# Token mixing of three batches beside the last MoE, and channel mixing over all tokens in chunks of 384

## The chip, the cores and the metric

The kernel runs on one core of one Trainium2 chip. The metric is the device time of one execution in microseconds (us), as the median of several runs. A profile of one execution stands beside it.

## The reference

Three layers follow each other on 4 batches of 576 tokens. Cut to what matters:

```python
attn = softmax(causal(q @ k.T / 8 + min(-(cum_i - cum_j), 0))) @ v      # 4 batches, 8 heads, 64 wide
x    = attn as (4, 576, 512)

xk, xr = mu_k * x + (1 - mu_k) * x_prev,  mu_r * x + (1 - mu_r) * x_prev
k = maximum(xk @ w_k, 0)                                                # 512 -> 1024
x = sigmoid(xr @ w_r) * (k * k @ w_v)                                   # the "MoE" layer

h = maximum(x.transpose(0, 2, 1) @ w_tok1, 0) @ w_tok2                  # token mixing: 576 -> 256 -> 576
u = x + h.transpose(0, 2, 1)
out = u + maximum(u @ w_ch1, 0) @ w_ch2                                 # channel mixing: 512 -> 1536 -> 512
```

All inputs are float32. Token mixing needs all 576 tokens of its batch; channel mixing works on each token by itself.

## The kernel before

**Precision.** Most products are made of two parts per operand, a rounded high part and the remainder. `products` (L103) issues three matmuls for each pair of 128-row blocks: high by high, high by low, low by high. So every result that a later product reads is "split": ScalarE writes the high part and VectorE or GpSimd subtracts it to make the low part. A weight is split the same way on its first use, in pieces: `weight_load` (L538) brings a piece of 256 or 288 columns into a buffer of the ring `xt`, and `weight_split` (L550) takes three ScalarE, two VectorE and one GpSimd instruction to place its two parts. The ring `xt_p` (L83) has six buffers; the attention's output of the batch in work lies in four of them until the MoE's `mix` has read it.

**Stages.** Attention runs over 32 heads in items. The MoE of each batch is cut into units (`moe_units`, L507): for each of two chunks of 256 and 320 tokens there are 8 `up`, 4 `gate` and 8 half `down` units. They are spread over the attention items that follow, so that TensorE has matmuls beside the softmax. The MoE of the last batch has no attention left beside it; its units and a few of the one before form the list `queue` (L734). The MoE's result goes to DRAM (`y_d`).

**The mixer.** For each batch, `load_y` brings the result back, `y_transpose` turns half of the 512 channels at a time (five PSUM tiles, each copied by ScalarE and subtracted by VectorE, and then one small copy by DMA for the 64 rows of the fifth block), `tok1` makes the hidden layer of token mixing (H1), and `tok2` the second product, adds x and splits the sum into `U`. `ch1` makes 12 blocks of the hidden layer of channel mixing for one chunk, `ch2` the four blocks of the output. Both work on the chunks of 256 and 320 tokens of one batch. The first of these steps, for batch 0, stand among the last units of `queue`, at places given in `st` (L836); the later batches' token steps stand between the channel steps of the batch before. All these PSUM tiles come from `ps_m` with six buffers; `ps_d`, with two, serves the earlier stages and the first 14 units of `queue`.

**Memory.** The tokens' second weight `T2`, the transposed `YN` and `H1` lie in the memory of the MoE's weight `WK`. `C1`, the first channel weight, has its own. The second channel weight takes the memory of `WV` and `WR`. `U` and the hidden layer take that of the MoE's `XR`, `KK` and `XK`.

**Order.** A planner orders the instructions of each engine by priorities and its own times. `at(place)` (L68) gives what stands under it the priority of that place in the list of attention items; a smaller number goes first. Buffers are handed out in the same order.

```python
    def at(place):
        return tc.high_priority(tc.cur_priority - int(place * 1000))
    ...
    xt_p = ctx.enter_context(tc.tile_pool(name="xt", bufs=6))
    ...
    ps_d = ctx.enter_context(tc.tile_pool(name="ps_d", bufs=2, space=PSUM, reuse_waits="tile"))
```

## Time and profile before

| what | value |
|---|---|
| median of 3 runs (lowest to highest) | 914.5 us (913.0 to 916.4) |
| the profiled execution: its time, its span | 911.6 us, 909.7 us |
| mean granted clock of TensorE in it | 0.989 |
| TensorE matmuls | 6032 |

The span runs from the first to the last instruction of the profiled execution; its time has 1.9 us more around it. PE is TensorE's matmuls, PEld its weight loads, DVE VectorE, ACT ScalarE, POOL GpSimd, SP SyncE, which issues nearly all DMAs. A line number is that of the kernel before; L108 is the matmul in `products`, which all products share. Matmuls overlap, so the time between two starts says more than the duration of one. The granted clock is 1.00 at 2.4 GHz and 0.50 at 1.2 GHz. A tile that lies in the memory of another carries its name: `t<-WK` is token mixing, `c<-XR,C` the first channel product, `c<-KK,WV` and `c<-XK,WR` the second.

### The profile page before, as it was taken

What the parts mean: (1) busy time and instruction counts of PE and PEld (TensorE: products, weight loads), DVE (VectorE), ACT (ScalarE), POOL (GpSimd) and SP (SyncE); (2) the same over time, 40 slices, a digit from 0 to 9 for tenths busy, and PEclk for the clock granted to TensorE, in tenths of its full rate; (3) what the DMA queues carried; (4) which work ended last, traced back from release to release, by engine and by line L of the source; (5) the groups of instructions that cost most, each with busy time, mean ns of one, the idle gap of its engine ahead of it and who ended that gap; (6) DMA issues with size and microseconds to landing.
All of it is one profiled execution on the core that took longest, in us unless ns stands there. A gap on an engine that the chain in (4) does not pass through costs nothing.

```text
span 909.7 us, 17091 instructions
## 1 busy us (share of the span) xinstructions
PE 871.0 (96%) x6032; PEld 793.3 (87%) x6032; DVE 523.3 (58%) x1582; ACT 468.1 (51%) x1296; POOL 292.1 (32%) x405
## 2 busy tenths in 40 slices
PE   7879999999899999999999799999999999999998
PEld 4435778998689989989999699999999999999998
DVE  5796776777898577876468887532323223222220
ACT  4787867766776757768367967321212111211120
POOL 4574536644565526545143734100000000000000
PEclk9979999999999999999999999999999999999999
DMA  7943355456644435542034553500010001000000
GB/s 200 246 126 88 91 142 115 108 120 153 146 95 102 107 94 125 107 109 42 32 94 144 177 175 128 166 4 22 10 52 4 15 16 50 6 16 15 19 6 30
DMA packets 57222, 79.61 MB, mean 88 GB/s; under 512 B 6144, under 2 KB 36096, under 8 KB 57136
## 3 DMA queue, kind: packets, MB, share of 16 engines
q1 hardware_dynamic: 55264, 77.92, 32.8%
q8 instruction: 48, 0.79, 0.4%
q10 hardware_dynamic: 1872, 0.59, 0.3%
q14 instruction: 38, 0.31, 0.1%
HBM read 46.67 MB, written 10.03 MB: 62 GB/s over the span
## 4 chain that ended last, share of the span: by engine, by line
PE 65%; DMA 10%; DVE 9%; issue 7%; ACT 5%; POOL 3%; SPq 0%; ACTq 0%; POOLq 0%; DVEq 0%
PE c L108 32%; PE vd L108 6%; PE h L108 5%; PE t L108 4%; PE r L108 3%; PE pv L446 3%; PE t L398 3%; PE pv L384 2%; DMA X<-HL 2%; DMA raw<-in_moe_w_ch_dram 2%; PE s L357 2%; PE s L276 2%; DVE raw L555 1%; PE s L277 1%; DMA HL<-in_qk_dram 1%
## 5 line engine op out<-in xcount | busy, mean ns | idle before, releaser
L108 PE MATMUL c<-XR,C 128*128 128x320 f32 (+1 forms) x1152 | 156.2, 295 | 1.0 <-ACT XR L809 1.0
L108 PEld LDWEIGHTS c<-XR,C 128*128 128x128 f32 x1152 | 153.2, 188 | 2.0 <-ACT XR L809 1.2
L264 POOL TENSOR_SCALAR P<-P,sum 64x576 f32<-64x576 f32 (+4 forms) x160 | 107.1, 673 | 120.7 <-DVE sum L263 64.0
L108 PE MATMUL h<-XK,WK 128*128 128x256 f32 (+1 forms) x768 | 121.7, 301 | 2.7 <-DVE XK L464 1.5
L108 PE MATMUL vd<-KK,WV 128*128 128x256 f32 (+1 forms) x768 | 121.1, 300 | 2.3 <-POOL KK L476 1.6
L261 ACT ACTIVATE P<-P,mx 64x576 f32<-64x576 f32 (+4 forms) x160 | 95.9, 600 | 31.1 <-DVE mx L251 27.0
L108 PEld LDWEIGHTS h<-XK,WK 128*128 128x128 f32 x768 | 105.5, 188 | 7.0 <-DVE XK L464 2.1
L108 PEld LDWEIGHTS vd<-KK,WV 128*128 128x128 f32 x768 | 105.3, 188 | 5.8 <-POOL KK L476 2.8
L108 PE MATMUL c<-KK,WV 128*128 128x256 f32 (+1 forms) x768 | 106.5, 294 | 0.1
L108 PEld LDWEIGHTS c<-KK,WV 128*128 128x128 f32 x768 | 103.0, 188 | 0.4 <-DVE XK L785 0.4
L784 ACT ACTIVATE KK<-c 128x256 fp32r<-128x256 f32 (+1 forms) x64 | 26.1, 409 | 145.9 <-PE c L108 145.9
L251 DVE CUSTOM_DVE_ANT_0 P<-s,maskc 64x288 f32<-64x288 f32 (+4 forms) x160 | 74.9, 474 | 19.3 <-PE t L398 4.7
L826 DVE TENSOR_TENSOR u<-c,u 128x256 f32<-128x256 f32 (+1 forms) x32 | 14.5, 457 | 121.7 <-PE c L108 121.7
L785 DVE SCALAR_TENSOR_TENSOR KK<-c,KK 128x256 fp32r<-128x256 f32 (+1 forms) x64 | 29.1, 457 | 66.8 <-ACT KK L784 66.8
L108 PE MATMUL r<-XR,WR 128*128 128x320 f32 (+1 forms) x384 | 62.3, 304 | 0.9 <-ACT k L473 0.6
L75 ACT ACTIVATE raw<-raw 128x256 f32<-128x256 f32 (+2 forms) x101 | 46.8, 464 | 27.8 <-DMA raw<-in_moe_w_ch_dram 11.3
L476 POOL TENSOR_TENSOR KK<-k,KK 128x256 fp32r<-128x256 f32 (+1 forms) x64 | 54.6, 857 | 19.1 <-ACT k L475 18.3
L555 DVE SCALAR_TENSOR_TENSOR raw<-raw 128x256 int32<-128x256 int32 (+2 forms) x85 | 47.0, 553 | 22.0 <-ACT raw L554 19.3
L108 PEld LDWEIGHTS r<-XR,WR 128*128 128x128 f32 x384 | 54.8, 193 | 2.4 <-ACT k L473 0.8
L108 PE MATMUL c<-XK,WR 128*128 128x320 f32 (+1 forms) x384 | 55.8, 294 | 0.0
L398 PE MATMUL t<-ident,P 128*128 128x128 f32 (+1 forms) x360 | 53.5, 262 | 1.8 <-DVE PT L424 1.3
L556 DVE SCALAR_TENSOR_TENSOR raw<-raw 128x256 int32<-128x256 int32 (+2 forms) x85 | 53.1, 628 | 1.1
(109 smaller groups left out, 1525.7 us busy)
## 6 DMA issues: line engine op xcount, KB each, us to landing
X<-HL SPq DMA_DIRECT2D x72, 288.0 KB
raw<-in_moe_w_ch_dram SPq DMA_DIRECT2D x48, 256.0 KB
HL<-in_qk_dram SPq DMA_DIRECT2D x12, 576.0 KB
yt<-y_d SPq DMA_DIRECT2D x16, 288.0 KB
raw<-in_moe_w_k_dram SPq DMA_DIRECT2D x8, 512.0 KB
...
```

Of the source, the lines that this page charges most:

```text
L75: nc.scalar.activation(out=out, in_=in_, func=AF.Copy, scale=scale)
L108: nc.tensor.matmul(ps, a, b, start=first and i == 0, stop=last and i == n - 1)
L251: nc.vector.tensor_tensor_reduce(out=P[0:m, c0:c1], in0=ps[0:m, 0:c1 - c0], in1=maskc[0:m, 512 - q0 + c0:512 - q0 + c1], scale=-scale, sca ...
L261: nc.scalar.activation(out=P[0:m, 0:w], in_=P[0:m, 0:w], func=AF.Exp, bias=mx[0:m, x:x + 1], scale=-1.0, accum_out=sm[0:m, 0:1])
L264: nc.gpsimd.tensor_scalar(out=P[0:m, 0:w], in0=P[0:m, 0:w], scalar1=sm[0:m, 1:2], scalar2=1.0, op0=ALU.mult, op1=ALU.mult)
L398: nc.tensor.transpose(ps[0:r, p0 + m * k:p0 + m * k + m], P[0:m, 128 * k:128 * k + r], ident[0:m, 0:m])
L446: nc.tensor.matmul(ps[:, o:n], vv[0:r, k, :], pair[t], start=(k == 0 and t == 0), stop=(k == nk - 1 and t == 1),)
L476: nc.gpsimd.tensor_tensor(out=kk[:, 1, m, 0:n], in0=t[:, 0:n], in1=f32(kk[:, 0, m, 0:n]), op=ALU.subtract)
L555: nc.vector.scalar_tensor_tensor(out=low, in0=high, scalar=3, in1=low, op0=ALU.logical_shift_left, op1=ALU.bitwise_or)
L556: nc.vector.scalar_tensor_tensor(out=low, in0=high, scalar=-2 ** 31, in1=low, op0=ALU.bitwise_and, op1=ALU.bitwise_or)
L784: nc.scalar.activation(out=hi, in_=ps, func=AF.Relu)
L785: nc.vector.scalar_tensor_tensor(out=lo, in0=ps, scalar=0.0, in1=f32(hi), op0=ALU.max, op1=ALU.subtract)
```

## The change

Channel mixing no longer goes batch by batch. All 2304 tokens form one row, cut into six chunks of 384 (`CH`), so that a chunk can hold tokens of two batches (`spans`). For this `tok2` no longer splits its sum into `U`: it adds into the tile of x and stores u to a new DRAM tensor, `u_d`. `split_u` loads the four blocks of a chunk and splits them; `ch2` loads each block again as the addend and stores its part of the output.

Token mixing of batches 0 and 1 is listed step by step (`tok_steps`) and spread over the units of the last MoE, from the seventh on, six places later than its unit. Token mixing of batch 2 stands behind the last unit, that of batch 3 between the `ch1` steps of the first chunk. All token steps take their PSUM tiles from `ps_d`. Batch 1's x lies in the ring `xt`, that of the other batches in five buffers of its own.

The first channel weight is in two parts: `C1A`, 512 columns, in its own memory, and `C1B`, 1024 columns, in that of `WK`. `T2`, `YN` and `H1` get memory of their own, and the hidden layer and `U` a new pool in the MoE's place. The pieces of the token weights and of `C1A` enter at one per unit from the start, those of `C1B` at two per unit with the last 12 units, those of the second channel weight behind batch 2's token steps and the first `ch1` steps.

```diff
@@ -99,6 +99,7 @@
     ext_d = dram.tile([G, 4, 2, S], F32, name="ext_d")
     y_d = dram.tile([B, DM, S], F32, name="y_d")
+    u_d = dram.tile([B, DM, S], F32, name="u_d")
@@ -693,7 +694,7 @@
-    ap = ctx.enter_context(tc.tile_pool(name="act", bufs=1, reuse_waits="tile"))
+    ap_s, ap = open_pool(name="act", bufs=1, reuse_waits="tile")
@@ -734,48 +735,50 @@
     queue = [(n, acts) for n in sorted(todo) for acts in todo[n]]
     att.close()
     with tc.using_default_side("right"):
         mx_p = ctx.enter_context(tc.tile_pool(name="mx", bufs=1, reuse_waits="tile"))
-        yt_p = ctx.enter_context(tc.tile_pool(name="yt", bufs=KD // 2, reuse_waits="tile"))
     ps_m = ctx.enter_context(tc.tile_pool(name="ps_m", bufs=6, space=PSUM, reuse_waits="tile"))
-    C1 = mx_p.tile([128, 2, KD, DC], F32R, name="C1")
+    CH = 384
+    CA = 512
+    DH = DM // 2
+    yt = {}
+    def load_y(b):
+        for p in range(KD):
+            if b == 1:
+                t = xt_p.tile([128, 1 + S], F32, tag="xt", name="yt")[:, 0:S]
+            else:
+                t = mx_p.tile([128, S], F32, tag="yt", name="yt", bufs=5)
+            nc.sync.dma_start(out=t, in_=y_d[b, 128 * p:128 * p + 128, :])
+            yt[b, p] = t
+    load_y(0)
+    C1A = mx_p.tile([128, 2, KD, CA], F32R, name="C1A")
+    T2 = mx_p.tile([128, 2, KT, S], F32R, name="T2")
     T1 = mx_p.tile([128, 2, NS, DT], F32R, name="T1")
+    YN = mx_p.tile([128, 2, NS, DH], F32R, name="YN")
+    H1 = mx_p.tile([128, 2, KT, DM], F32R, name="H1")
+    C1B = WK.rearrange("p (t k f) -> p t k f", t=2, k=KD)
     c2a = WV.rearrange("p (t k f) -> p t k f", t=2, f=DM)
     c2b = WR.rearrange("p (t k f) -> p t k f", t=2, f=DM)
-    o = 0
-    T2 = WK[:, o:o + 2 * KT * S].rearrange("p (t k f) -> p t k f", t=2, k=KT)
-    o += 2 * KT * S
-    DH = DM // 2
-    YN = WK[:, o:o + 2 * NS * DH].rearrange("p (t k f) -> p t k f", t=2, k=NS)
-    o += 2 * NS * DH
-    H1 = WK[:, o:o + 2 * KT * DM].rearrange("p (t k f) -> p t k f", t=2, k=KT)
-    U = act["XR"]
-    def hid(t, k, n):
-        return act["KK"][:, t, k, 0:n] if k < KF else act["XK"][:, t, k - KF, 0:n]
+    def c1(t, k, m):
+        f = 128 * m
+        return C1A[:, t, k, f:f + 128] if f < CA else C1B[:, t, k, f - CA:f - CA + 128]
 
     def c2(t, k, ms):
         return c2a[:, t, k, ms] if k < KF else c2b[:, t, k - KF, ms]
-    yt = {}
-    def load_y(b):
-        for p in range(KD):
-            if p < KD // 2:
-                t = yt_p.tile([128, S], F32, tag="yt", name="yt")
-            else:
-                t = xt_p.tile([128, 1 + S], F32, tag="xt", name="yt")[:, 0:S]
-            nc.sync.dma_start(out=t, in_=y_d[b, 128 * p:128 * p + 128, :])
-            yt[p] = t
 
     def y_transpose(b, h):
         for i in range(NS):
             r = min(128, S - 128 * i)
-            ps = ps_m.tile([128, DH], F32, tag="d", name="yn")
+            ps = ps_d.tile([128, DH], F32, tag="d", name="yn")
             for p in range(KD // 2):
-                nc.tensor.transpose(ps[0:r, 128 * p:128 * p + 128], yt[h * (KD // 2) + p][:, 128 * i:128 * i + r], ident)
+                nc.tensor.transpose(ps[0:r, 128 * p:128 * p + 128], yt[b, h * (KD // 2) + p][:, 128 * i:128 * i + r], ident)
             nc.scalar.activation(out=YN[0:r, 0, i, :], in_=ps[0:r, :], func=AF.Copy)
             nc.vector.tensor_tensor(out=YN[0:r, 1, i, :], in0=ps[0:r, :], in1=f32(YN[0:r, 0, i, :]), op=ALU.subtract)
         nc.sync.dma_start(out=f32(YN[TAIL:2 * TAIL, 0, NS - 1, :]), in_=f32(YN[0:TAIL, 1, NS - 1, :]))
@@ -786,7 +789,7 @@
 
     def tok1(b, h):
         for m in range(KT):
-            ps = ps_m.tile([128, DH], F32, tag="d", name="t1")
+            ps = ps_d.tile([128, DH], F32, tag="d", name="t1")
             ms = slice(128 * m, 128 * m + 128)
             k = NS - 1
             products(ps, [(T1[:, 0, k, ms], T1[:, 1, k, ms], YN[:, 0, k, :], YN[:, 1, k, :]) for k in range(k)], last=False)
@@ -795,36 +798,53 @@
             ds = slice(DH * h, DH * h + DH)
             relu_split(ps, H1[:, 0, m, ds], H1[:, 1, m, ds])
 
-    ut = {}
-    def tok2(b, c):
-        cs = slice(*CHS[c])
-        n = width(c)
-        u = sm_p.tile([128, KD, n], F32, tag=f"u{c}", name="u")
+    def tok2(b, m):
+        ms = slice(128 * m, 128 * m + 128)
+        t = yt.pop((b, m))
+        for cs in (slice(0, S // 2), slice(S // 2, S)):
+            ps = ps_d.tile([128, S // 2], F32, tag="d", name="t2")
+            products(ps, [(H1[:, 0, k, ms], H1[:, 1, k, ms], T2[:, 0, k, cs], T2[:, 1, k, cs]) for k in range(KT)])
+            nc.vector.tensor_tensor(out=t[:, cs], in0=ps, in1=t[:, cs], op=ALU.add)
+        nc.sync.dma_start(out=u_d[b, ms, :], in_=t)
+    def tok_steps(b):
+        return [(load_y, b), (y_transpose, b, 0), (tok1, b, 0), (y_transpose, b, 1), (tok1, b, 1)] + [(tok2, b, m) for m in range(KD)]
+    def spans(i):
+        r, o = [], 0
+        while o < CH:
+            b, a = divmod(CH * i + o, S)
+            z = min(S, a + CH - o)
+            r.append((b, a, z, o))
+            o += z - a
+        return r
+    def load_u(i, m):
+        t = xt_p.tile([128, 1 + S], F32, tag="xt", name="ut")[:, 0:CH]
+        for b, a, z, o in spans(i):
+            nc.sync.dma_start(out=t[:, o:o + z - a], in_=u_d[b, 128 * m:128 * m + 128, a:z])
+        return t
+    def split_u(i):
         for m in range(KD):
-            ms = slice(128 * m, 128 * m + 128)
-            ps = ps_m.tile([128, n], F32, tag="d", name="t2")
-            products(ps, [(H1[:, 0, k, ms], H1[:, 1, k, ms], T2[:, 0, k, cs], T2[:, 1, k, cs]) for k in range(KT)])
-            nc.vector.tensor_tensor(out=u[:, m, 0:n], in0=ps, in1=yt[m][:, cs], op=ALU.add)
-            nc.scalar.activation(out=U[:, 0, m, 0:n], in_=u[:, m, 0:n], func=AF.Copy)
-            nc.vector.tensor_tensor(out=U[:, 1, m, 0:n], in0=u[:, m, 0:n], in1=f32(U[:, 0, m, 0:n]), op=ALU.subtract)
-        ut[b, c] = u
-    def ch1(c, m):
-        n = width(c)
+            t = load_u(i, m)
+            nc.scalar.activation(out=U[:, 0, m, :], in_=t, func=AF.Copy)
+            nc.vector.tensor_tensor(out=U[:, 1, m, :], in0=t, in1=f32(U[:, 0, m, :]), op=ALU.subtract)
+    def ch1(m):
+        ps = ps_m.tile([128, CH], F32, tag="d", name="c1")
+        products(ps, [(c1(0, k, m), c1(1, k, m), U[:, 0, k, :], U[:, 1, k, :]) for k in range(KD)])
+        relu_split(ps, HID[:, 0, m, :], HID[:, 1, m, :])
+    def ch2(i, m):
         ms = slice(128 * m, 128 * m + 128)
-        ps = ps_m.tile([128, n], F32, tag="d", name="c1")
-        products(ps, [(C1[:, 0, k, ms], C1[:, 1, k, ms], U[:, 0, k, 0:n], U[:, 1, k, 0:n]) for k in range(KD)])
-        relu_split(ps, hid(0, m, n), hid(1, m, n))
-    def ch2(b, c, m):
-        n = width(c)
-        ms = slice(128 * m, 128 * m + 128)
-        ps = ps_m.tile([128, n], F32, tag="d", name="c2")
-        products(ps, [(c2(0, k, ms), c2(1, k, ms), hid(0, k, n), hid(1, k, n)) for k in range(KC)])
-        u = ut[b, c]
-        nc.vector.tensor_tensor(out=u[:, m, 0:n], in0=ps, in1=u[:, m, 0:n], op=ALU.add)
-        nc.sync.dma_start(out=out[b, ms, CHS[c][0]:CHS[c][1]], in_=u[:, m, 0:n])
+        t = load_u(i, m)
+        ps = ps_m.tile([128, CH], F32, tag="d", name="c2")
+        products(ps, [(c2(0, k, ms), c2(1, k, ms), HID[:, 0, k, :], HID[:, 1, k, :]) for k in range(KC)])
+        nc.vector.tensor_tensor(out=t, in0=ps, in1=t, op=ALU.add)
+        for b, a, z, o in spans(i):
+            nc.sync.dma_start(out=out[b, ms, a:z], in_=t[:, o:o + z - a])
 
     def by_columns(pieces):
         return [p[x] for x in range(len(pieces[0])) for p in pieces]
@@ -832,62 +852,64 @@
     wq = []
     for k in range(NS):
         wq += weight(T1[:, 0, k:k + 1], T1[:, 1, k:k + 1], w_tok1, k)
-    wq += by_columns([weight(C1[:, 0, k:k + 1], C1[:, 1, k:k + 1], w_ch1, k) for k in range(KD)])
-    st = [14, 7, 5, 4, 1]
-    START = {}
-    for q, f in zip(st, ([load_y, 0], [y_transpose, 0, 0], [tok1, 0, 0], [y_transpose, 0, 1], [tok1, 0, 1])):
-        START.setdefault(q, []).append(f)
-    done = 0
+    for k in range(KT):
+        wq += weight(T2[:, 0, k:k + 1], T2[:, 1, k:k + 1], w_tok2, k)
+    wq += by_columns([weight(C1A[:, 0, k:k + 1], C1A[:, 1, k:k + 1], w_ch1[:, 0:CA], k) for k in range(KD)])
+    fill = tok_steps(0)[1:] + tok_steps(1)
+    nf = len(fill)
+    n0 = 6
     for x, (n, acts) in enumerate(queue):
-        if len(queue) - x == KF + KD:
-            for k in range(KT):
-                for p in weight(T2[:, 0, k:k + 1], T2[:, 1, k:k + 1], w_tok2, k):
-                    with at(N0 + n + 0.6):
-                        p()
+        left = len(queue) - x
+        if left == KF + KD:
+            wq += by_columns([weight(C1B[:, 0, k:k + 1], C1B[:, 1, k:k + 1], w_ch1[:, CA:], k) for k in range(KD)])
         if x == 14:
             act["ps"] = ps_m
         with at(N0 + n + 0.5):
             run(acts)
-            for f in START.get(len(queue) - x, []):
-                f[0](*f[1:])
-        if done <= x and wq:
-            done += 1
-            with at(N0 + n + 0.6):
-                wq.pop(0)()
+        for _ in range(1 if left > KF + KD else 2):
+            if wq:
+                with at(N0 + n + 0.6):
+                    wq.pop(0)()
+        while x >= n0 and fill and nf - len(fill) < nf * (x - n0 + 1) // (len(queue) - n0):
+            with at(N0 + n + 6):
+                run(fill[0:1])
+            fill.pop(0)
+    run(fill)
     st_s.close()
-    sm_p = ctx.enter_context(tc.tile_pool(name="sm2", bufs=1, reuse_waits="tile"))
-    ctx.enter_context(at(N0 + n + 2))
-    tok2(0, 0)
+    ap_s.close()
+    ch_p = ctx.enter_context(tc.tile_pool(name="ch", bufs=1, reuse_waits="tile"))
+    HID = ch_p.tile([128, 2, KC, CH], F32R, name="HID")
+    U = ch_p.tile([128, 2, KD, CH], F32R, name="U")
+    ctx.enter_context(at(N0 + n + 7))
     two = []
     for k in range(KC):
         W, kk = (c2a, k) if k < KF else (c2b, k - KF)
         two.append(weight(W[:, 0, kk:kk + 1], W[:, 1, kk:kk + 1], w_ch2, k))
     wq += by_columns(two)
-    for b in range(B):
+    def convert(n):
+        for _ in range(n):
+            if wq:
+                wq.pop(0)()
+    fill = tok_steps(2)
+    for f in fill:
+        run([f])
+        convert(1)
+    split_u(0)
+    last = tok_steps(3)
+    for i in range(B * S // CH):
         for m in range(KC):
-            ch1(0, m)
-            for _ in range(2):
-                if wq:
-                    wq.pop(0)()
-        tok2(b, 1)
+            ch1(m)
+            convert(2)
+            if i == 0 and m > 1 and last:
+                run([last.pop(0)])
+        run(last)
+        last = []
+        if i + 1 < B * S // CH:
+            split_u(i + 1)
         for m in range(KD):
-            ch2(b, 0, m)
-        if b + 1 < B:
-            load_y(b + 1)
-            y_transpose(b + 1, 0)
-        for m in range(KC):
-            ch1(1, m)
-            if b + 1 < B:
-                if m == 2:
-                    tok1(b + 1, 0)
-                if m == 3:
-                    y_transpose(b + 1, 1)
-                if m == 6:
-                    tok1(b + 1, 1)
-        if b + 1 < B:
-            tok2(b + 1, 0)
-        for m in range(KD):
-            ch2(b, 1, m)
+            ch2(i, m)
 
 # ---- launch: one core; inputs and outputs as the reference has them ----
```

## Rows read from the trace of the kernel before

**Rows 1.** The page's first part: busy time, share of span, instructions per engine.

```profile
PE 871.0 (96%) x6032; PEld 793.3 (87%) x6032; DVE 523.3 (58%) x1582; ACT 468.1 (51%) x1296; POOL 292.1 (32%) x405
```

**Rows 2.** The table of windows: busy by engine, granted clock, DMA share, GB/s.

```profile
460.00:480.00 20.00, 18.37 (x152) 17.55 (x151) 14.66 (x27) 14.25 (x42) 11.57 (x14) 1.00 0.24 69
...
505.00:510.00 5.00, 3.60 (x23) 3.07 (x21) 4.91 (x6) 4.54 (x15) 4.32 (x6) 1.00 0.34 100
510.00:515.00 5.00, 4.74 (x31) 4.36 (x31) 4.00 (x8) 5.00 (x17) 3.61 (x4) 1.00 0.56 179
515.00:520.00 5.00, 1.95 (x11) 1.26 (x10) 4.93 (x8) 5.00 (x17) 4.26 (x6) 0.89 0.46 127
520.00:525.00 5.00, 4.76 (x19) 4.33 (x18) 2.89 (x8) 3.15 (x9) 2.58 (x4) 0.50 0.83 243
```

**Rows 3.** TensorE's timeline, 456 to 547: start, us, instruction, count, idle before.

```profile
456.61 4.25 PE L108 MATMUL h<-XK,WK 128*128 128x256 f32 x36
...
516.77 0.44 PE L778 MATMUL yn<-ident,yt 128*128 128x128 f32 x2 [1.62 <-ACT e L488]
...
546.66 17.25 PE L108 MATMUL c<-XR,C 128*128 128x256 f32 x144 [0.97 <-ACT XR L809]
```

**Rows 4.** TensorE's timeline, 602 to 679: token and channel mixing.

```profile
602.80 1.58 PE L108 MATMUL t<-WK,T 128*128 128x256 f32 x12
...
606.90 8.97 PE L108 MATMUL c<-XR,C 128*128 128x320 f32 x60
...
615.70 3.04 PE L108 MATMUL t<-WK 128*128 128x256 f32 x24
...
618.58 3.69 PE L108 MATMUL c<-KK,WV 128*128 128x320 f32 x24
...
639.70 17.25 PE L108 MATMUL c<-XR,C 128*128 128x256 f32 x144
...
656.79 3.67 PE L108 MATMUL t<-WK 128*128 128x320 f32 x24
...
660.30 2.99 PE L108 MATMUL c<-KK,WV 128*128 128x256 f32 x24
...
677.27 1.25 PE L778 MATMUL yn<-ident,yt 128*128 128x128 f32 x10
...
678.28 5.53 PE L108 MATMUL c<-XR,C 128*128 128x320 f32 x36
```

**Rows 5.** TensorE's timeline during attention: score matmuls of 384 columns.

```profile
304.11 0.34 PE L276 MATMUL s<-X 128*128 128x384 f32 x1
...
304.46 1.63 PE L108 MATMUL h<-XK,WK 128*128 128x320 f32 x10
```

**Rows 6.** Groups by line and shape, ScalarE and VectorE, 440 to 910.

```profile
L75 ACT ACTIVATE raw<-raw 128x256 f32<-128x256 f32 x51 | 22.2, 435 | 18.0 <-DMA raw<-in_moe_w_ch_dram 11.3 <-DMA raw<-in_moe_w_tok_dram 4.9 <-POOL WV L560 1.6
...
L779 ACT ACTIVATE WK<-yn 128x256 fp32r<-128x256 f32 x32 | 10.2, 388 | 38.9 <-PE yn L778 38.9
...
L780 DVE TENSOR_TENSOR WK<-yn,WK 128x256 fp32r<-128x256 f32 x32 | 11.6, 413 | 0.6 <-ACT WK L779 0.6
```

**Rows 7.** The weight tiles' view: duration min/median/max, first and last start.

```profile
L560 POOL TENSOR_TENSOR C<-raw,C x24: 730/833/1034, 470.9 to 521.7; 128x256 fp32r<-128x256 f32 x24
```

**Rows 8.** ScalarE's timeline, the first and the last of five transpose evictions.

```profile
518.29 0.36 ACT L779 ACTIVATE WK<-yn 128x256 fp32r<-128x256 f32 x1
...
520.67 0.36 ACT L779 ACTIVATE WK<-yn 64x256 fp32r<-64x256 f32 x1
```

**Rows 9.** The view of the tile y_d: loads into yt.

```profile
L768 SPq DMA_DIRECT2D yt<-y_d x16: 319/327/423, 446.7 to 752.6; - x16
```

**Rows 10.** SyncE's queue waits after 420: us in total, times, longest.

```profile
SPq L827 <- DVE u L826: 235.6, 31, 26.1
```

**Rows 11.** GpSimd's timeline: last step of first and fifth channel-weight piece.

```profile
470.94 0.77 POOL L560 TENSOR_TENSOR C<-raw,C 128x256 fp32r<-128x256 f32 x1 [0.89 <-POOL T L560]
...
485.92 0.86 POOL L560 TENSOR_TENSOR C<-raw,C 128x256 fp32r<-128x256 f32 x1 [1.47 <-ACT C L75]
```

10 lines of the change are left out of this document (5 added, 5 removed).

## The prediction, before the result was known

> **What bounds the kernel now.** I read the page first. TensorE is busy 96% of the span and no other engine reaches 60% [rows 1]. That share counts overlapping matmuls, so I went to the table of windows for the part that the change touches: everything after about 440 us, when attention drains [rows 2]. From 460 to 480 TensorE loses 1.63 us. From 505 to 525 it loses 4.95 us (1.40, 0.26, 3.05, 0.24), and the granted clock falls to 0.89 and 0.50 in and after the window in which TensorE was busy only 1.95 of 5 us. ScalarE is busy 5.00 of 5 us from 510 to 520, VectorE about 4.9 in two of the four windows. So here the last MoE is held by ScalarE and VectorE. The timeline names the stalls: a transpose waits 1.62 us for a PSUM buffer that ScalarE's tanh has not emptied, and the first channel product 0.97 us for U [rows 3]. After that, TensorE's own stream sets the end: its groups follow each other without a gap [rows 4].
>
> The clock has its price too. In 520 to 525 TensorE is busy 4.76 us at 0.50 (1.2 of 2.4 GHz), which loses 2.4 us, and 515 to 520 loses 0.2. Idle plus clock is 1.63 + 4.95 + 0.97 + 2.6 = **10.2 us**. That is all that better overlap can return, unless the matmuls themselves become cheaper.
>
> **The wider chunk.** Channel mixing issues 288 matmuls per chunk: 8 chunks of 256 and 320 before (2304), 6 of 384 after (1728). The columns are the same: 663,552. Start to start, 144 matmuls of 256 columns take 17.09 us in the first product (639.70 to 656.79) and 16.97 in the second (660.30 to 677.27), 144 of 320 take 21.12 (618.58 to 639.70), and 60 of 320 take 8.80 [rows 4]. That is 0.118 and 0.1467 us each, 0.460 and 0.458 ns per column: proportional, with almost no part per instruction. The nearest rows for 384 columns are score matmuls: a pair takes 0.35 us (304.11 to 304.46), 0.175 each, and the hundredths in which the rows stand allow 0.18 [rows 5]. A batch now costs 17.09 + 16.97 + 2 x 21.12 = 76.3 us, four 305.2. At 0.458 ns per column 384 costs 0.176, and 1728 of them 304.1. Bounds: 0.18 gives 311.0 (+5.8). If what 320 columns take beyond 2.4 GHz (146.7 - 133.3 = 13.4 ns) were one fixed amount per matmul, 384 would cost 173.4 and the sum 299.6 (-5.6). I take **-1**, because the 384 rows, at 0.175, lie with the proportional value.
>
> The Trainium skill, page "TensorE: Matmul & The Clock Gate", section "Wait — 56ns, not 53.3ns?", has a fixed floor of about 2.5 ns per warm matmul beside N / 2.4 GHz. By it alone 576 fewer matmuls would save an estimated 1.4 us. Our rows show ten per cent over N / 2.4 GHz at every width, not a constant; the trace disagrees, and I use the rows.
>
> **Token mixing of batch 1 moves beside the last MoE.** One batch costs TensorE: two transposing passes of 1.0 us (677.27 to 678.28), four groups of the first product (two take 602.80 to 606.90, so 2.05 each), and the second product at 2.9 + 3.5 (615.70 to 618.58, 656.79 to 660.30) [rows 4]: 16.6 us. The new halves of 288 hold the same columns. Moving this work is worth nothing by itself, since it filled TensorE without idle where it stood. It is worth what it fills. Also, the last MoE gets less ScalarE work at its tightest place: a weight piece takes three activations of some 0.43 us, 1.3 in all [rows 6]. Before, 24 pieces of the first channel weight were converted from 470.9 to 521.7 [rows 7], right through the second chunk's up projections. After, nothing is queued there between the 17 pieces of the token weights and the first third of the channel weight, and the last 12 units, when the rest enters at two per unit. So I expect most of 505 to 525 back: of 7.5 us (4.95 idle, 2.6 clock) I take 5.4, of the 1.63 before it half, and the 0.97, the wait for the first U, whole: **-7.2**. Bounds: all 10.2, or nothing if the engines stay as full with batch 1's evictions.
>
> **What the move adds.** All token steps now share the two buffers of ps_d, where before they drew on six. A transposing step occupies a buffer for two transposes (0.2), a ScalarE copy 0.388 and a VectorE subtraction 0.413 [rows 6]; with two buffers a pass of five lasts at least 2.5 us for 1.0 of TensorE. Where ScalarE is full the copies follow each other every 0.6 us (five from 518.29 to 520.67) [rows 8], so a pass lasts about 3. Batches 0, 1 and 3 have cover: the MoE's matmuls, or the first chunk's channel products. Batch 2 stands between the last down projection and the first channel product, and the only cover is that product itself, which needs U. U's loads stand in program order behind nine pieces of the second channel weight and all of the first. So its two passes lie bare: 2 x 2, plus 0.8 for an eviction by both engines (0.388 + 0.413) before its second product may start: **+5**. Bounds: 0 if U comes in time, 9 if ScalarE's and VectorE's queues double the evictions.
>
> **The round trip through DRAM.** It adds 16 stores of u and 64 loads (eight spans per 128 rows, four row blocks, read twice), all on SP: 80 x 0.33 us [rows 9] over 350 us in which SP mostly sleeps. What waits is the store of u, for VectorE's addition; behind it on SP stand weight loads and u loads. The output stores already wait so, 235.6 us in sum [rows 10], and TensorE loses nothing by it. In each later chunk U is rewritten during the second product, 144 x 0.176 = 25 us for four tiles of about 1 us each, and an addition has six PSUM buffers of slack. I take 0; with no cover it would be about 3 us a chunk.
>
> **The end.** The last addition works on 384 columns instead of 320. VectorE takes 0.413 us for 256 [rows 6], so 64 more cost about 0.1, and I give the larger store as much again: +0.2.
>
> **Sum.** -1 - 7.2 + 5 + 0.2 = -3.0 us against the profiled execution's 911.6 (span 909.7, 1.9 around it): 908.6. The median of the runs is 914.5, 2.9 above that execution; on that scale **911.5**.
>
> **The rivals.**
> *All of it is filled.* If U is ready when batch 2 starts, ch1(0) fills its gaps and the 5 us don't come; with 10.2 returned and 1 from the matmuls that is -11, 903.5. For it: the old kernel's first batch had its chain covered except for those stalls. Against: the order of U's loads. Chance 0.24.
>
> *The xt ring starves the converters (the other side).* load_y(1) takes four of the six xt buffers until u of batch 1 is stored, so the remaining 16 pieces of the first channel weight go through two. When the old kernel had two free (four held x of the last batch), the first and the fifth piece of this weight came out at 470.94 and 485.92 [rows 11], 3.75 us apart on average. Sixteen from about 505 end near 561; nine pieces of the second weight at the old pace with more buffers (the other 19 of 24 pieces until 521.7 [rows 7], 1.88 each) put U near 578. TensorE's work to the end of batch 2 (240 matmuls per chunk, 28.3 + 35.2, and 3 x 16.6) takes from 456.6 [rows 3] to 570. The price is 8 us of waiting, some 2 more for half clock, 2 for late first pieces of the second weight and 2 that remain of batch 2's own gaps: -1 - 7.2 + 14 + 0.2 = +6, 920. It decides once the first c1 matmul starts more than about 8 us after batch 2's last second product. For it: the measured pace. Against: batch 1's buffers come free before that, and gaps inside batch 2 absorb part. Chance 0.22.
>
> *The gaps only move.* Returned and added stalls cancel to within 2 us: 914. Chance 0.16.
>
> *A fixed cost per matmul.* If the 13.4 ns are per instruction, another 4.6 us go: 906. The 384-column rows speak against it. Chance 0.05.
>
> **How the numbers follow.** My forecast, 911.5 with 908 to 914 as its own range, has the remaining 0.33. About 0.5% (4.6 us) is what a measurement of this kernel can tell from no change. Faster: 0.24 + 0.05 + 0.10 of my forecast = 0.39. Slower: 0.20 of the ring's 0.22. Same: the remaining 0.41. The range from 901 to 921 takes in both outer cases; what is left out is a converter stall longer than priced, or a gain in the part before 440.
>
> **What would show it.** Right: c1 matmuls at 0.176 us start to start; windows between 500 and 530 with TensorE over 4.5 of 5 and the clock at 1.00; a dip at batch 2's transposes between 545 and 580. Wrong: c1 at 0.173 or less (the fixed cost); no dip (all filled); a single idle stretch before the first c1 (the ring); a stall at chunk borders (the round trip, costed at nothing); a different time before 440.

## The result, and the profile after

The change made the kernel slower: 926.07 us, median of 4 runs (925.25 to 931.05), against 914.88 for the kernel before (913.0 to 916.4). The ratio is 1.0135, with a 95% interval of 1.0094 to 1.0175. The prediction, 911.5 with 901 to 921, had the wrong sign and its range did not hold the time. The profiled execution took 925.25 us, 923.2 of them span, so 13.5 us more span than before. From here on line numbers are those of the changed kernel, but for rows of the kernel before, e15 and e18: L109 is the matmul of `products`, L781 a token transposition, L782 and L783 its two evictions by ScalarE and VectorE, and L75, L555, L556, L557, L75 and L561 are the six steps on a weight piece; L832 is ScalarE's half of the split of U (L836 in e13).

The page's first part answers to [rows 1]: nothing in the shares points to a cause. All engines but TensorE are a little less busy.

```profile
PE 873.6 (95%) x5456; PEld 791.8 (86%) x5456; DVE 513.9 (56%) x1542; ACT 465.2 (50%) x1264; POOL 290.5 (31%) x405
```

The windows do. First three windows of the kernel before, which cover the last MoE and the first channel products (columns as in [rows 2]):

```profile
456.00:500.00 44.00, 42.37 (x336) 41.55 (x335) 32.91 (x70) 31.43 (x91) 18.09 (x22) 1.00 0.38 117
500.00:550.00 50.00, 43.80 (x279) 39.96 (x279) 42.23 (x81) 40.63 (x120) 28.45 (x35) 0.93 0.55 172
550.00:600.00 50.00, 49.91 (x400) 48.89 (x399) 28.40 (x69) 25.58 (x74) 12.53 (x16) 1.00 0.38 123
```

The same windows of the changed kernel, a narrow one, and two late ones:

```profile
456.00:500.00 44.00, 39.11 (x302) 36.21 (x301) 27.91 (x62) 28.60 (x82) 14.55 (x18) 0.96 0.30 93
500.00:550.00 50.00, 46.47 (x309) 44.24 (x308) 24.89 (x59) 29.05 (x82) 19.46 (x23) 0.97 0.55 163
550.00:600.00 50.00, 39.92 (x232) 35.66 (x231) 35.86 (x77) 30.81 (x89) 15.26 (x19) 0.86 0.56 170
...
560.00:570.00 10.00, 8.00 (x40) 6.94 (x41) 5.05 (x11) 4.12 (x12) 2.76 (x4) 0.70 0.34 102
...
700.00:800.00 100.00, 100.00 (x575) 100.00 (x575) 21.84 (x40) 15.76 (x32) 0.00 (x0) 1.00 0.16 48
800.00:900.00 100.00, 100.00 (x575) 100.00 (x575) 19.83 (x36) 13.77 (x28) 0.00 (x0) 1.00 0.12 36
```

Before, TensorE idles 1.63 + 6.20 + 0.09 = 7.9 us here and loses 3.5 to the clock (0.07 of 50). After, it idles 4.89 + 3.53 + 10.08 = 18.5 us and loses 0.04 x 44 + 0.03 x 50 + 0.14 x 50 = 10.3. That is 28.8 against 11.4, **17.4 us worse**. From 700 to 900 TensorE is busy in every microsecond, at full clock. So nearly all of the loss lies between 456 and 600, and the second place to look at is what the matmuls gave back.

Starts of a chunk's first product in TensorE's timeline, after (they answer to [rows 4]):

```profile
768.97 8.48 PE L109 MATMUL c<-U,C1A 128*128 128x384 f32 x48
...
819.21 8.48 PE L109 MATMUL c<-U,C1A 128*128 128x384 f32 x48
```

A chunk of 288 matmuls lasts 50.24 us, 0.1744 each; six chunks are 301.4 us against 305.2 before: **-3.8**. 17.4 - 3.8 = 13.6 us, and the span grew by 13.5. The account closes, within the 0.7 us that clocks in hundredths leave open over 144 us.

Who stalls TensorE is in its timeline. These are four of its idle times (in square brackets, with what ended them), and the start of the first channel product, which was a wait of 0.97 in [rows 3] and is none here:

```profile
534.22 0.44 PE L781 MATMUL yn<-ident,yt 128*128 128x128 f32 x2 [1.78 <-DVE YN L783]
...
540.25 0.41 PE L781 MATMUL yn<-ident,yt 128*64 128x128 f32 x2 [1.26 <-DVE YN L783]
...
558.14 0.44 PE L781 MATMUL yn<-ident,yt 128*128 128x128 f32 x2 [1.66 <-DVE YN L783]
561.19 0.63 PE L781 MATMUL yn<-ident,yt 128*64 128x128 f32 x2 [2.60 <-DVE YN L783]
...
588.80 0.87 PE L109 MATMUL c<-U,C1A 128*128 128x384 f32 x4
```

A token transposition waits for a PSUM buffer that VectorE's subtraction (L783) has not yet read, because ScalarE's copy (L782) came late. Why it was late is in ScalarE's timeline, just ahead of 540.25:

```profile
534.14 0.37 ACT L782 ACTIVATE YN<-yn 128x256 fp32r<-128x256 f32 x1
537.45 0.43 ACT L75 ACTIVATE raw<-raw 128x256 f32<-128x256 f32 x1 [2.94 <-DMA raw<-in_moe_w_ch_dram]
537.79 0.41 ACT L555 ACTIVATE raw<-raw 128x256 uint32<-128x256 uint32 x1
538.59 0.44 ACT L75 ACTIVATE raw<-raw 128x256 f32<-128x256 f32 x1 [0.39 <-DMA raw<-in_moe_w_ch_dram]
538.93 0.42 ACT L555 ACTIVATE raw<-raw 128x256 uint32<-128x256 uint32 x1
539.25 0.37 ACT L782 ACTIVATE YN<-yn 128x256 fp32r<-128x256 f32 x1
```

ScalarE works through its list in order. From 534.51 to 537.45 it stands idle at a weight piece whose load has not landed, and the next PSUM eviction, which needs no weight, stands two pieces behind it. VectorE stands the same way at its half of the piece. The table of waits from 430 to 640 puts sums to this (us, times, longest):

```profile
DVE raw L556 <- ACT raw L555: 41.6, 23, 4.0
ACT raw L75 <- DMA raw<-in_moe_w_ch_dram: 36.1, 30, 2.9
...
PE yn L781 <- DVE YN L783: 12.4, 9, 2.6
```

The same table of the kernel before:

```profile
DVE raw L555 <- ACT raw L554: 15.4, 16, 2.4
ACT raw L75 <- DMA raw<-in_moe_w_ch_dram: 11.3, 16, 1.4
```

Why the loads are late is in the chain that ended last. Between two loads of the same buffer it runs through the buffer itself:

```profile
542.36 3.17 DMA raw<-in_moe_w_ch_dram
545.61 0.43 ACT raw L75
546.04 0.33 ACT raw L555
546.45 0.44 DVE raw L556
546.91 0.88 DVE raw L557
547.81 0.44 ACT WK L75
...
548.32 0.76 POOL WK L561
549.10 2.72 DMA raw<-in_moe_w_ch_dram
```

One turn is 549.10 - 542.36 = 6.74 us, and two of the six ring buffers take part: four hold x of batch 1, loaded from 505.27 on. That makes 3.4 us per piece, and GpSimd's last step on the sixteen pieces of C1B starts from 517.6 to 568.8, which answers to the 24 of [rows 7], at 470.9 to 521.7. SyncE, which issues the loads, waits 26.0 us for that step from 500 to 600, 15 times: so it is the buffer that a load waits for.

### The profile page after: what moved, and what is told of

It is laid out like the page before. It is cut to its first block, busy times and chain, and to the rows that moved or that the text cites. A ratio compares the mean times of both kernels' runs of the same rounds, so it can differ in the third digit from the quotient of the medians.

```text
span 923.2 us, 16023 instructions
## 1 busy us (share of the span) xinstructions
PE 873.6 (95%) x5456; PEld 791.8 (86%) x5456; DVE 513.9 (56%) x1542; ACT 465.2 (50%) x1264; POOL 290.5 (31%) x405
## 4 chain that ended last, share of the span: by engine, by line
PE 64%; DMA 12%; DVE 10%; ACT 5%; issue 5%; POOL 3%; SPq 0%; ACTq 0%; POOLq 0%; DVEq 0%
PE c L109 31%; PE vd L109 7%; PE h L109 6%; DMA raw<-in_moe_w_ch_dram 4%; PE t L109 3%; PE pv L447 3%; PE r L109 3%; PE t L399 3%; PE pv L385 2%; DMA X<-HL 2%; DMA ext_d<-e 2%; PE s L358 2%; PE s L277 1%; PE s L278 1%; DVE t L463 1%
## 5 line engine op out<-in xcount | busy, mean ns | idle before, releaser
L265 POOL TENSOR_SCALAR P<-P,sum 64x576 f32<-64x576 f32 (+4 forms) x160 | 106.9, 673 | 118.4 <-DVE sum L264 63.4
L787 ACT ACTIVATE HID<-c 128x384 fp32r<-128x384 f32 x72 | 35.4, 491 | 193.3 <-PE c L109 193.3
L109 PE MATMUL h<-XK,WK 128*128 128x256 f32 (+1 forms) x768 | 123.8, 302 | 4.1 <-DVE YN L783 2.1
L109 PE MATMUL vd<-KK,WV 128*128 128x256 f32 (+1 forms) x768 | 122.1, 301 | 0.0
L109 PEld LDWEIGHTS h<-XK,WK 128*128 128x128 f32 x768 | 106.3, 189 | 9.2 <-DVE YN L783 2.5
L109 PEld LDWEIGHTS vd<-KK,WV 128*128 128x128 f32 x768 | 106.3, 189 | 2.8 <-DVE t L463 0.4
L109 PE MATMUL c<-HID,WV 128*128 128x384 f32 x576 | 106.0, 337 | 0.0
L109 PE MATMUL c<-U,WK 128*128 128x384 f32 x576 | 104.3, 337 | 0.0
L109 PEld LDWEIGHTS c<-HID,WV 128*128 128x128 f32 x576 | 100.4, 188 | 0.1
L109 PEld LDWEIGHTS c<-U,WK 128*128 128x128 f32 x576 | 100.2, 188 | 0.3
L788 DVE SCALAR_TENSOR_TENSOR HID<-c,HID 128x384 fp32r<-128x384 f32 x72 | 40.0, 556 | 85.6 <-ACT HID L787 85.6
L845 DVE TENSOR_TENSOR ut<-c,ut 128x384 f32<-128x384 f32 x24 | 13.4, 557 | 115.4 <-PE c L109 115.4
L75 ACT ACTIVATE raw<-raw 128x256 f32<-128x256 f32 (+2 forms) x101 | 47.0, 466 | 48.9 <-DMA raw<-in_moe_w_ch_dram 36.1
L556 DVE SCALAR_TENSOR_TENSOR raw<-raw 128x256 int32<-128x256 int32 (+2 forms) x85 | 43.9, 517 | 46.7 <-ACT raw L555 44.8
L109 PE MATMUL r<-XR,WR 128*128 128x320 f32 (+1 forms) x384 | 63.0, 301 | 0.0
L109 PEld LDWEIGHTS r<-XR,WR 128*128 128x128 f32 x384 | 54.9, 191 | 0.7
L109 PE MATMUL c<-HID,WR 128*128 128x384 f32 x288 | 54.7, 336 | 0.0
L557 DVE SCALAR_TENSOR_TENSOR raw<-raw 128x256 int32<-128x256 int32 (+2 forms) x85 | 53.5, 630 | 1.2
```

The lines of the kernel that those rows point to most:

```text
L75: nc.scalar.activation(out=out, in_=in_, func=AF.Copy, scale=scale)
L109: nc.tensor.matmul(ps, a, b, start=first and i == 0, stop=last and i == n - 1)
L265: nc.gpsimd.tensor_scalar(out=P[0:m, 0:w], in0=P[0:m, 0:w], scalar1=sm[0:m, 1:2], scalar2=1.0, op0=ALU.mult, op1=ALU.mult)
L556: nc.vector.scalar_tensor_tensor(out=low, in0=high, scalar=3, in1=low, op0=ALU.logical_shift_left, op1=ALU.bitwise_or)
L557: nc.vector.scalar_tensor_tensor(out=low, in0=high, scalar=-2 ** 31, in1=low, op0=ALU.bitwise_and, op1=ALU.bitwise_or)
L787: nc.scalar.activation(out=hi, in_=ps, func=AF.Relu)
```

## The experiments

Times are medians; ratios are to the kernel before, measured alongside (913.7 to 914.6 us). Edits are against the changed kernel, but for e15 and e18. Profiled executions are compared with care: attention, which the edits but for e10's leave alone, ended as much as 8.5 us later in some of them (the last start of its copy L408 is 436.8 in the changed kernel and 445.3 in e11).

**The two suspects, and both together.** e1 gives the token steps six PSUM buffers, e2 holds batch 1's x in its own memory so that the ring has six buffers, e3 is both, e4 changes the chunk alone.

```diff
 # e1, in y_transpose, tok1 and tok2
-ps = ps_d.tile([128, DH], F32, tag="d", name="yn")
+ps = ps_m.tile([128, DH], F32, tag="d", name="yn")
 # e2, in load_y
-            if b == 1:
+            if b == 4:
 # e4
-CH = 384
+CH = 288
```

e1: 

> The changed kernel with one thing undone: the token steps take their PSUM tiles from the six buffers that the MoE and channel products use, not from the two of ps_d. Theory A (the two buffers are what holds TensorE at the transposes): the waits of transposes for VectorE's subtraction, 12.4 us in the changed kernel, fall under 3 us, the half-clock stretches with them, and the time falls from 926 to 912 to 915. Theory B (ScalarE, which works in order, stands behind weight pieces whose loads are late because batch 1 holds four of the six ring buffers; the two PSUM buffers only pass it on): ScalarE's waits for weight loads stay near 36 us, the stall shows up as a wait for YN at the next product instead, and the time falls by less than 5 us, to 921 or more.

e2: 

> The changed kernel with one thing undone: batch 1's x lies in the five buffers of the other batches instead of the ring of the weight pieces, so it is loaded a little later. Theory B: ScalarE's waits for weight loads fall from 36 to under 15 us, the transposes no longer wait for late copies, and the time falls from 926 to 912 to 917. Theory A: ScalarE's waits fall, but the transposes with two PSUM buffers still wait about 10 us, and the time stays above 921.

e3: 

> Both edits at once: six PSUM buffers for the token steps and no batch in the ring. If A and B are two halves of one stall, this is the first to go clearly below either alone: 908 to 912, with at most 8 us of TensorE idle between 456 and 620 (19 in the changed kernel). If a third cause holds it (batch 2's token steps have nothing beside them, whatever the buffers), it stays at 915 or more and the idle lies between 555 and 590.

e4: 

> The changed kernel with chunks of 288 tokens instead of 384: eight chunks, 2304 channel matmuls instead of 1728, the same columns. Theory of proportional cost: matmuls start every 0.132 us and the time stays within 2 us of the changed kernel's 926 in the channel part. Theory of a fixed cost per matmul (13 ns): 576 more matmuls cost 7.5 us, and the time rises to 933.

Measured: e1 920.21, 1.0063 [1.0037, 1.0088]; e2 918.11, 1.0036 [1.0015, 1.0057]; e3 917.64, 1.0036 [1.0013, 1.0058]; e4 931.76, 1.0182 [1.0135, 1.0229]. So either half returns 6 to 9 us, and both together no more than the second alone; e1 and e2 lie between the ranges of their two theories. Windows and waits of e1 show what the buffers do and what they don't:

```profile
456.00:500.00 44.00, 43.94 (x360) 42.67 (x359) 35.61 (x83) 30.92 (x92) 15.64 (x19) 1.00 0.46 144
500.00:550.00 50.00, 46.09 (x312) 44.09 (x310) 22.16 (x52) 29.83 (x84) 19.45 (x24) 0.97 0.46 139
550.00:600.00 50.00, 40.85 (x248) 38.02 (x248) 36.56 (x81) 30.99 (x90) 18.01 (x22) 0.86 0.66 212
...
ACT raw L75 <- DMA raw<-in_moe_w_ch_dram: 31.5, 26, 4.8
PE yn L781 <- ACT k L474: 3.9, 3, 1.5
...
PE yn L781 <- DVE e L505: 2.4, 1, 2.4
```

Before 500 six buffers clear the loss: TensorE idles 0.06 us where it idled 4.89. From 500 to 600 it still idles 13.1 us, against 13.6. There ScalarE waits for loads nearly as long, and TensorE waits for other things that ScalarE and VectorE make between the pieces: the relu of an up projection (k), that of the token steps, VectorE's e. In e2 ScalarE's wait falls to 16.4, and TensorE's for L783 from 12.4 to 7.1. In e3 ScalarE's is 22.1; the pieces come earlier (C1B at 507.7 to 534.1) and crowd the second chunk's up projections: TensorE is busy 4.42 of 10 us from 510 to 520, which gives back what the two halves would add up to. In e4 a chunk lasts 38.13 us, 0.1324 per matmul, so the matmuls of its eight chunks take 305.0 us, 3.6 more than at 384. Two of its starts:

```profile
773.71 6.56 PE L109 MATMUL c<-U,C1A 128*128 128x288 f32 x48
811.84 6.56 PE L109 MATMUL c<-U,C1A 128*128 128x288 f32 x48
```

The medians differ by 5.7, and the intervals allow either. That is more than the one theory of e4 and less than the other.

**The pieces themselves.** e12 leaves out the 16 pieces of C1B and the 24 of the second channel weight, e17 only the 24. e18 leaves out the same 24 in the kernel before, and e15 gives that kernel's token steps the two PSUM buffers.

```diff
 # e12 alone
-            wq += by_columns([weight(C1B[:, 0, k:k + 1], ...
 # e12, e17 and (in the kernel before) e18
-    wq += by_columns(two)
 # e15, in the kernel before: yn, t1 and t2
-            ps = ps_m.tile([128, DH], F32, tag="d", name="yn")
+            ps = ps_d.tile([128, DH], F32, tag="d", name="yn")
```

e12: 

> The changed kernel without the 16 pieces of the first channel weight that enter late and the 24 of the second: it leaves their loads and splits out, and the channel products read what the MoE's weights left in that memory, so the output is not the reference's. Two PSUM buffers and batch 1 in the ring stay. Theory B (ScalarE's queue stands behind pieces whose loads are late): the stalls between 520 and 600 go nearly whole, the time falls from 926 to 908 to 913. Theory A (two PSUM buffers by themselves): at least 8 us of transposes waiting for VectorE's subtraction stay, and the time is 918 or more.

e17: 

> The changed kernel without the 24 pieces of the second channel weight alone (it leaves their loads and splits out, and the second channel product reads the MoE's weights, so the output is not the reference's); the 16 late pieces of the first stay. Without both kinds the time fell by 20 us. If the pieces that meet token steps beside the MoE (the first weight's) hold the engines, most of the loss up to 560 stays and the time is 914 to 920; if those behind the MoE (the second weight's) do, it is 908 to 912.

e18: 

> The old kernel without the 24 pieces of the second channel weight (left out in the same way). There they stand beside channel products that fill TensorE. Theory: pieces cost only where TensorE's next work hangs on ScalarE or VectorE; so leaving them out gains at most 3 us here, 911 to 914, against the gain in the changed kernel. If they cost by themselves, the time falls to 908 or less.

e15: 

> The old kernel with one part of the change: all token steps take their PSUM tiles from the two buffers of ps_d. Theory A at full strength (two buffers cost by themselves, 6 to 9 us as between the changed kernel and its six-buffer twin): 919 to 922, with waits of transposes for VectorE's subtraction. Theory that they cost only where ScalarE's queue is late: batches 1 to 3, beside channel products and an empty ScalarE, lose nothing, batch 0 a little: 914 to 917.

Measured: e12 906.15, 0.9918 [0.9889, 0.9946]; e17 919.92, 1.0059 [1.0034, 1.0084]; e18 911.34, 0.9958 [0.9936, 0.9981]; e15 921.54, 1.0084 [1.0058, 1.0111]. Without both sets of pieces (e12) the changed order takes less time than the kernel before. That kernel converts all of its pieces, though; without its second set it takes 911.34, and without the pieces of its first weight it was not run. The windows of e12 show where its 20 us came back:

```profile
456.00:500.00 44.00, 39.82 (x307) 37.52 (x306) 25.05 (x56) 26.57 (x78) 16.55 (x20) 0.96 0.35 111
500.00:550.00 50.00, 50.00 (x345) 48.70 (x344) 19.89 (x49) 23.11 (x60) 12.07 (x13) 0.97 0.37 115
550.00:600.00 50.00, 49.21 (x313) 47.77 (x312) 19.72 (x42) 13.89 (x32) 0.00 (x0) 1.00 0.26 81
```

From 500 to 600 TensorE stands 0.8 us, against 13.6 in the changed kernel, with the same two PSUM buffers. Of the 20 us some 6 belong to the second weight (926.07 to 919.92) and 14 to C1B (919.92 to 906.15). In the old order the second weight's pieces cost 3 us (914.4 to 911.3). What stays in e12 is the loss before 500, where the pieces of the token weights still come, and which e1 cleared.

e15 shows that two buffers cost the old order 8 us too (913.7 to 921.5), and where. Its windows, and two of its waits:

```profile
500.00:550.00 50.00, 38.99 (x235) 34.11 (x233) 38.56 (x71) 39.45 (x116) 30.21 (x37) 0.90 0.54 168
550.00:600.00 50.00, 49.54 (x394) 49.46 (x395) 30.59 (x69) 24.64 (x71) 12.04 (x15) 0.97 0.40 127
...
536.61 0.44 PE L778 MATMUL yn<-ident,yt 128*128 128x128 f32 x2 [2.90 <-DVE WK L785]
...
540.48 1.11 PE L778 MATMUL yn<-ident,yt 128*128 128x128 f32 x4 [2.51 <-DVE WK L780]
```

The time is that of e15's first theory, the place that of its second: all of it is batch 0, beside the last MoE and the pieces of the first channel weight. Which of those two neighbours it is, e15 does not separate. Batches 1 to 3, beside channel products with next to no pieces, leave TensorE 0.5 us idle from 550 to the last product. Two buffers are enough there.

**Where the batches stand.** e16 puts batches 0 and 1 beside the last MoE and batches 2 and 3 beside the first two chunks; e7 puts only batch 0 there and one batch beside each of three chunks. Both have e3's edits. e8 is e7 with C1B at one piece per unit; in it the last four pieces of the second channel weight are converted only after the first chunk's second product has read their place.

```diff
 # e16 (e7 moves batch 1 as well, and keeps batch 0 at its places)
-    fill = tok_steps(2)
-    for f in fill:
-        run([f])
-        convert(1)
     split_u(0)
-    last = tok_steps(3)
     for i in range(B * S // CH):
+        last = tok_steps(i + 2) if i + 2 < B else []
 # e8, beside e7
-        for _ in range(1 if left > KF + KD else 2):
+        for _ in range(1):
```

e7: 

> Six PSUM buffers, ring free, and token mixing of batch 0 alone beside the last MoE; those of batches 1, 2 and 3 stand between the first products of channel chunks 0, 1 and 2. The chunks of 384 over all tokens stay. Theory: the move of batches 1 and 2 out of the channel stage, where nothing was idle, is what costs; with cover for every later batch only the stall of the last MoE remains (10 us, as in the old kernel), less 3 us for the wider chunk: 909 to 913. If the wider chunk or the trip of u through DRAM cost something by themselves, 917 or more.

e8: 

> As the run before, and the last two thirds of the first channel weight enter at one piece per unit, not two, in the last 12 units of the MoE. If ScalarE's burst of weight pieces is what stalls the last MoE's second chunk, the loss between 500 and 550 falls by 3 to 6 us and the time to 904 to 909. If those pieces are drawn forward into idle buffers whatever their place, no change.

e16: 

> Token mixing of batches 0 and 1 beside the last MoE as in the changed kernel, six PSUM buffers and the ring free; batch 2's steps moved from behind the last MoE in between the first products of channel chunk 0, batch 3's into chunk 1. Batch 1's second product then covers the wait for U's memory, and batch 2 has channel products beside it. If those two waits are what is left after six buffers and a free ring, the stretch 550 to 600 loses 4 us or less (10.7 with both edits alone) and the time is 909 to 913, below the old kernel. If the weight pieces hold ScalarE and VectorE whatever stands beside, it is 915 to 920.

Measured: e7 918.47, 1.0056 [1.0032, 1.0079]; e8 920.11, 1.0070 [1.0040, 1.0101]; e16 920.04, 1.0052 [1.0028, 1.0076]. None brought the hoped gain. e8 and e16 came out as their second theories had it; e7 lies where its text would blame the wider chunk or the trip through DRAM, but TensorE idles only 0.3 us from 600 to 900 in it. With batch 2 off the path, the wait that the ring rival had named appears, in e7 in a single piece:

```profile
549.88 1.65 PE L109 MATMUL c<-U,C1A 128*128 128x384 f32 x4 [9.55 <-ACT U L832]
```

In e16 it is 6.20 us at 570.79. In both the ring is free of batch 1, so the four held buffers are not what makes this wait.

**U earlier.** Since U now seemed the wait, e5, e6 and e11 split the first chunk's U ahead of batch 2's steps (e6 and e11 with e3's edits); e9 (on e7), e10 and e11 place U in memory that is free early; e10 also gives the ring a seventh buffer, for one of the five of x; e13 and e14 (on e9) split the first U straight from batch 0's tiles, e14 with pieces spread otherwise.

```diff
 # e5, e6, e11
+    split_u(0)
     for f in fill:
         run([f])
         convert(1)
-    split_u(0)
 # e9, e10, e11, e13, e14: U ahead of HID in the pool
+    U = ch_p.tile([128, 2, KD, CH], F32R, name="U")
     HID = ch_p.tile([128, 2, KC, CH], F32R, name="HID")
-    U = ch_p.tile([128, 2, KD, CH], F32R, name="U")
 # e13, e14, in split_u
-            t = load_u(i, m)
+            t = first_u.pop(m)[:, 0:CH] if i == 0 else load_u(i, m)
```

e5: 

> The changed kernel with one line moved: the first chunk's U is loaded and split ahead of batch 2's token steps and of the second channel weight's pieces, not behind them. Theory C (batch 2's steps have nothing beside them, because the first channel product waits for U, and U's loads stand behind nine weight pieces): channel matmuls appear between 555 and 590, TensorE's idle there falls from about 10 us to under 4, and the time falls from 926 by 6 to 10 us. If C is not a cause, or the first channel product then waits for other things (ring buffers still held by batch 1), the time stays above 923.

e6: 

> Six PSUM buffers, ring free of batch 1, and U first. If A, B and C together are the whole loss, the stretch from 550 to 600 loses under 3 us (10.7 without U first) and the time is 906 to 911, below the old kernel's 914. If the converters of the weights are the limit in themselves (ScalarE full from 510 to 530), the loss only moves and the time stays at 915 to 919.

e9: 

> The run with one batch beside the last MoE (six PSUM buffers, ring free, later batches between channel products), and U allocated ahead of the hidden layer, so that it lies in the memory of XK and XR, which the gates leave before the last down projections, and not in that of KK and the gate tiles. That run had one wait of 9.5 us before the first channel product, for U's copy, which ScalarE made only after the last gate tile was stored. Theory: this wait goes, ring buffers come free sooner, and the time falls from 918 to 907 to 911, below the old kernel's 914. Rival: ScalarE's queue, with weight pieces whose loads are late at its head, delays the copy whatever its memory; then at least 6 us of the wait stay and the time is 915 or more.

e10: 

> The same with a ring of seven buffers instead of six, paid for by four instead of five buffers for x of the mixer. Theory B (late weight loads at the head of ScalarE's queue): ScalarE's waits for weight loads, 19.5 us with one batch, fall under 13 us, and the time falls another 2 to 4 us below the run before. If the queue is not what holds it now, the two are equal within 2 us.

e11: 

> Batches 0 to 2 beside and behind the last MoE as in the changed kernel, with six PSUM buffers, the ring free, U loaded first and U in the memory of XK and XR. Theory C (batch 2's token steps lie bare because the first channel product waits for U): channel matmuls now run between the last down projection and 590, the stretch 560 to 590 loses under 4 us (11.4 with U first but high), and the time is 908 to 913. If it stays at 917 or more, something else than U keeps the channel products from filling batch 2's gaps.

e13: 

> One batch beside the last MoE, six PSUM buffers, ring free, U low, and the first chunk's U split straight from batch 0's tiles, without the trip through DRAM, so that no u load takes ring buffers before the first channel product. Theory B: the ring serves the weight pieces with all six buffers, ScalarE's queue moves, the wait for U (8.1 us in the run before this edit) falls under 2 us, and the time goes from 920 to 909 to 913. If ScalarE is still held by late loads at that place, it stays at 917 or more.

e14: 

> The run before, with the late pieces of the first channel weight at one per unit instead of two and three pieces per channel step afterwards. If ScalarE's load from 510 to 530 is what is left, the stretch 520 to 530 loses under 1 us (2 to 4 in the earlier runs of this kind) and the time is 906 to 911; if pieces are drawn forward anyway, no change against the run before.

Measured:

```
e5  923.78  1.0104 [1.0085, 1.0123]      e11 918.26  1.0029 [1.0001, 1.0057]
e6  918.15  1.0039 [1.0012, 1.0065]      e13 920.21  1.0082 [1.0056, 1.0108]
e9  922.47  1.0071 [1.0043, 1.0100]      e14 922.67  1.0099 [1.0065, 1.0133]
e10 924.36  1.0108 [1.0076, 1.0140]
```

This theory fell: no version gains over its base, e3 or e7, and e5 gains 2 us over the changed kernel, within the intervals. ScalarE's timeline of e9 shows what stands ahead of U:

```profile
543.19 0.43 ACT L75 ACTIVATE raw<-raw 128x256 f32<-128x256 f32 x1 [2.47 <-DMA raw<-in_moe_w_ch_dram]
...
543.84 0.42 ACT L489 ACTIVATE e<-r 128x320 f32<-128x320 f32 x1
...
550.48 0.43 ACT L75 ACTIVATE raw<-raw 128x256 f32<-128x256 f32 x1 [2.27 <-DMA raw<-in_moe_w_ch_dram]
...
551.13 1.34 ACT L832 ACTIVATE U<-ut 128x384 fp32r<-128x384 f32 x3
```

The tanh at 543.84 belongs to matmuls that ended at about 535. It stood behind pieces; so the last y went out at 548.17, and U's copies, from 551.13 on, stood behind two more pieces. Whether U's memory would have been free earlier is not shown: ScalarE comes to the copies without a wait of their own. In e13 the loads are prompt, and the wait is longer still:

```profile
ACT raw L75 <- DMA raw<-in_moe_w_ch_dram: 10.3, 15, 1.8
...
553.13 1.65 PE L109 MATMUL c<-U,C1A 128*128 128x384 f32 x4 [10.89 <-ACT U L836]
```

From 430 to 640 ScalarE waits less for loads there than in the kernel before (11.3). From 542 to 552.5 it is busy 7.56 us, nearly all of it with pieces, and comes to U's copies at 552.57, straight from a piece. So a late load is not needed: pieces that are there on time hold the copies as well. Whatever memory or order U has, it is in the same queues.

## Why the prediction was wrong

**The step that failed is "Batches 0, 1 and 3 have cover", in "What the move adds": it put the stalls of token steps beside the last MoE at nothing.** Most of what "Token mixing of batch 1 moves beside the last MoE" wanted back did come back, at the place that it named. Where the kernel before lost 7.5 us from 505 to 525, the changed one idles 0.17 us from 500 to 530, at full clock, and the first channel product does not wait:

```profile
510.00:520.00 10.00, 10.00 (x73) 10.00 (x72) 3.35 (x8) 8.35 (x23) 7.56 (x11) 1.00 0.57 167
520.00:530.00 10.00, 9.83 (x70) 9.57 (x69) 3.85 (x8) 4.91 (x13) 4.13 (x5) 1.00 0.59 181
```

But TensorE idles 4.9 us from 456 to 500 and 8.6 from 530 to 575, while batches 0 and 1 are in work: 13.7 us where the forecast had none, and most of the loss to the clock. Batch 3 has the cover: TensorE is full from 640 to 900.

Behind it stands what "Token mixing of batch 1 moves beside the last MoE" took for granted. It counted what ScalarE has to do, and there it was right: from 500 to 550 ScalarE is busy 29.05 us against 40.63. It assumed that an engine with less work is an engine that answers sooner. The sixteen pieces of C1B were put into the same 12 units as the token steps, at a time when four of six ring buffers are held, so each piece stood waiting at the head of ScalarE's list, and the evictions behind it. Waiting for loads rose from 11.3 to 36.1 us while the busy share fell. The MoE's matmuls are cover only until their own evictions stand behind the same piece. e1 puts the part before 500 on the two buffers, e12 nearly all of the rest on the late pieces: the same steps, the same PSUM buffers, without the 16 pieces of C1B and the 24 of the second weight, and the time is 906.15.

How much of that is the pieces' waiting and how much their work is not settled. e12 takes away both. A free ring gives 8 us of the 20 (e2), and six PSUM buffers add nothing to it (e3), though ScalarE's wait is down to 22.1; e13, whose loads are prompt, still takes 920.21. What the runs show is that pieces ahead of evictions in one list cost, late or prompt.

**The +5 for batch 2 was met by luck.** I priced two bare passes of some 3 us. In the trace one pass lies bare, from 575.75 to 583.16, more than twice as long, with 4.8 us of TensorE idle; the second stands beside the first channel product, since U came in time, and costs nothing. Against the forecast's -7.2 + 5 = -2.2 for the stalls, the trace has +17.4.

**The wider chunk: -1 forecast, -3.8 measured**, within the bounds of -5.6 and +5.8. The direction held in e4. The score matmuls at 0.175 were the right row; I rounded away from them to 0.176, and the measured 0.1744 is nearer to the rival with a fixed part (0.1734). The time given for that rival, 906, should read 907 (911.5 - 4.6).

**The round trip through DRAM and the chunk borders: nothing, as forecast.** TensorE is full from 700 to 900. The part before 440 did not move either.

**The ring rival was right in its sign and in how the pieces become late, not in place or size.** It had 3.75 us per piece (3.4 measured), the last piece near 561 (568.8) and the first channel product waiting 8 us for U. In the changed kernel that product does not wait. The late pieces held back the evictions ahead of it, batch by batch, and by 588.80 U had long caught up. Only when batch 2 was moved off the path (e7, e16) did the single wait appear, 9.55 and 6.2 us, and there without the held buffers. Its stalls, -7.2 + 14 = +6.8 us, fall well short of the +17.4, so 926 lies beyond its 920, and beyond the range, which by the prediction's own words leaves out "a converter stall longer than priced". And the tell-tale that I had named, one idle stretch ahead of the first channel product, would have misled.

**What stays open.** No version that converts all pieces beats the kernel before; e2, e3 and e11 come nearest, 0.36% [0.15, 0.57], 0.36% [0.13, 0.58] and 0.29% [0.01, 0.57] slower. The kernel before without the pieces of its first channel weight was not run, so what any order would gain from their absence is not known. A version that loads C1B before batch 1's x, or that keeps pieces out of the lists of ScalarE and VectorE until their load has landed, was not tried. Why e14 and e10 are a little worse than their bases is not settled. That the pieces stand early because the schedule assumes a prompt load is only argued.
